# Hash attention and a gated feed-forward on one core: the feed-forward of a batch placed inside the attention of the next, with DMA transposes of the operands and weights cast by DMA

## The chip, the cores and the metric

The kernel runs on one core of one Trainium2 chip. The metric is device time in microseconds (us); less is better. A time is one execution on the chip; the median of three is given with its lowest and highest. One execution was also taken by the hardware profiler, and all durations come from that one. PE is TensorE, DVE is VectorE, ACT is ScalarE, POOL is GpSimd, SP is SyncE, from which most DMAs are issued.

## The reference, cut to what matters

Attention of 4 batches x 8 heads, 768 tokens, 64 dims; a score counts only where query and key fall into the same bucket, which is given by the signs of 6 projections. Then a gated feed-forward over all 3072 tokens.

```python
q_bits = einsum('bhsd,dk->bhsk', q, proj) > 0        # the same for k; proj is 64 x 6
mask = bucket(q_bits)[:, :, :, None] == bucket(k_bits)[:, :, None, :]
scores = where(mask, q @ k.T / sqrt(64), -1e9)
attn = softmax(scores) @ v                            # 4 x 8 x 768 x 64
x = attn.transpose(0, 2, 1, 3).reshape(3072, 512)
ffn = (gelu(x @ w_gate) * (x @ w_val)) @ w_out        # 512 -> 1536 -> 512
out = x + sigmoid(x @ w_res) * ffn
```

## The kernel before, in words

The mask costs no comparison. Six bit rows of plus or minus one half and one constant row stand under the 64 dims of each operand, so that a matmul over 71 rows gives the scaled score and, where any bit differs, a large negative amount beside it; the exponential then gives zero. The exponential's scale puts the size right, so q is divided by 2048 when it is copied.

A pair is two heads of a batch; there are 16 pairs, worked in groups of two. `prep` (L120) makes the operands of a group. For each pair and side it loads 384 KB of float32 (L128), transposes six 128x128 blocks on PE into PSUM (L137), copies them to SBUF with DVE (L139) and casts the two heads' halves into the operand tile `aug`, one half on POOL (L144) and one on DVE (L145). The values are loaded, cast to bfloat16 with a column of ones beside them, and summed over tokens on POOL (L147 to L158). Bit matmuls of all four operands of the group go to four column strips of PE (L166), DVE makes signs of them (L169), and 16 small DMAs carry seven rows each under the operands (L176).

`attn` (L189) works a pair in nine chunks. A chunk has 1024 score columns in two PSUM banks (L212), one exponential of 128 x 1024 (L217) and eight value matmuls of 65 columns (L230). Each head is opened by a matmul of 390 columns that adds a tiny multiple of the value sums (L223) and closed by a reciprocal and a product on DVE (L201, L202), which write `x_tok`. After each batch `xpose` transposes `x_tok` to `x_sb`, 24 blocks on PE, with copies on DVE (L242, L244).

Weights are loaded in float32 tiles on SP and cast on POOL (L94, L97), three pieces a group from the second group on. When all attention is done, the PSUM pools are closed and the feed-forward runs over six blocks of 512 tokens: for each of 12 slices of the hidden width four matmuls for the gate (L276), gelu on ACT (L279), four for the value (L282) and a product on DVE (L284); then for each 128 tokens four matmuls for the residual gate (L288), a tanh (L291), twelve output matmuls (L294), two DVE instructions (L298, L299) and a store (L301).

The order on each engine is made by a scheduler from dependences and priorities, and each engine runs its own list strictly in that order. A `tile` of a pool waits for a free buffer of its tag.

Of the kernel before, what the change touches and what calls it, by code (L numbers as in the profile page):

```python
# [18 lines left out]
def kernel(  # L19
# [12 lines left out]
    nc = tc.nc  # L32
    B, H, S, D = q.shape
    NBITS = proj.shape[1]
    NTOK = B * S
# [7 lines left out]
    NPAIR = B * HP  # L43
    NROW = NBITS + 1
    assert D == 64 and S == 768 and NBITS <= 15
# [10 lines left out]
    ident = const.tile([P, P], FP32, name="ident")  # L56
    make_identity(nc, ident)
    ident_bf = const.tile([P, P], BF16, name="ident_bf")
    nc.vector.tensor_copy(ident_bf, ident)
    eps_sb = const.tile([P, P], BF16, name="eps_sb")  # L60
    nc.vector.memset(eps_sb, EPS)

    projw = const.tile([P, 32], FP32, name="projw")
    nc.vector.memset(projw, 0.0)
    nc.sync.dma_start(projw[0:D, 0:NBITS], proj)
    nc.sync.dma_start(projw[D:2 * D, NROW:NROW + NBITS], proj)

    cst = const.tile([P, 1], FP32, name="cst")
    nc.gpsimd.memset(cst, -0.5)
    for j in range(4):  # L70
        for hi in range(2):
            nc.gpsimd.affine_select(
                out=cst, in_=cst, compare_op=ALU.not_equal,
                fill=(1.0 if j % 2 == 0 else -NBITS / 4.0),
                base=-(32 * j + hi * NROW + NBITS), pattern=[[0, 1]], channel_multiplier=1)

    x_tok = const.tile([P, B * T, DMODEL], BF16, name="x_tok")
    x_sb = const.tile([P, KM, NTOK], BF16, name="x_sb")

    w_pool = ctx.enter_context(tc.tile_pool(name="w", bufs=1))  # L80
    wst_pool = ctx.enter_context(tc.tile_pool(name="wst", bufs=2))
    wts = {}

    def load_w(ap, kdim, ndim, name):
        t = w_pool.tile([P, kdim // P, ndim], BF16, name=name)
        wts[name] = t
        per = DFF // ndim
        todo = []
        for k0 in range(0, kdim // P, per):
            n = min(per, kdim // P - k0)  # L90

            def go(k0=k0, n=n):
                tmp = wst_pool.tile([P, per, ndim], FP32, tag="wtmp", name="wtmp")
                nc.sync.dma_start(  # L94
                    tmp[:, :n, :],
                    ap[k0 * P:(k0 + n) * P, :].rearrange("(o p) n -> p o n", p=P))
                nc.gpsimd.tensor_copy(t[:, k0:k0 + n, :], tmp[:, :n, :])  # L97
            todo.append(go)
        return todo

    wload = (load_w(moe_w_gate, DMODEL, DFF, "wg") + load_w(moe_w_val, DMODEL, DFF, "wv")
             + load_w(moe_w_res, DMODEL, DMODEL, "wr") + load_w(moe_w_out, DFF, DMODEL, "wo"))

    with ExitStack() as actx:
        ld_pool = actx.enter_context(tc.tile_pool(name="ld", bufs=3))
        aug_pool = actx.enter_context(tc.tile_pool(name="aug", bufs=4))
        t32_pool = actx.enter_context(tc.tile_pool(name="t32", bufs=5))
        va_pool = actx.enter_context(tc.tile_pool(name="va", bufs=4))
        bit_pool = actx.enter_context(tc.tile_pool(name="bit", bufs=2))
        e_pool = actx.enter_context(tc.tile_pool(name="e", bufs=12))  # L110
        sm_pool = actx.enter_context(tc.tile_pool(name="sm", bufs=2))
        misc_ps = actx.enter_context(tc.tile_pool(name="misc_ps", bufs=2, space=PSUM))
        sc_ps = actx.enter_context(tc.tile_pool(name="sc_ps", bufs=2, space=PSUM))
        av_ps = actx.enter_context(tc.tile_pool(name="av_ps", bufs=2, space=PSUM))

        CH = [(0, 4), (4, 2)]
        KA = D + NROW
        vaug, aug = {}, {}
# [213 lines left out]
```

## Time and profile before

| | us |
|---|---|
| median of 3 runs | 423.8 |
| lowest, highest | 420.07, 426.41 |
| the profiled execution | 423.37 |
| its span, first to last instruction | 421.1 |

Mean granted TensorE clock over the span: 0.986 of 2.4 GHz. The profile gives each engine's busy time, groups of instructions by line and shape, the waits, and the chain of work that ended last. Ends of matmuls are modelled and overlap with the next ones, so a rate of PE is read from the starts. The idle time behind a row, with the engine that ended it, stands in brackets.

### The profile page before, as it was taken

How to read it: one execution, taken by the hardware profiler on the slowest of the kernel's cores; microseconds unless marked ns; L12 is line 12 of the kernel's file. 1: busy time of each engine (PE TensorE's matmuls, PEld its weight loads, DVE VectorE, ACT ScalarE, POOL GpSimd, SP SyncE). 2: the span in 40 equal slices, each digit the busy share in tenths (PEclk: the TensorE clock that was granted, in tenths of full speed). 3: DMA queues.
4: the chain of work that ended last, by engine and by line, in shares of the span. 5: the costliest groups of instructions: out<-in, count | busy, mean ns of one | idle time of the engine just before them, and what ended most of it. 6: DMA issues, size and time to landing. Idle time of an engine off the chain costs nothing.

```text
span 421.1 us, 7282 instructions
## 1 busy us (share of the span) xinstructions
PE 381.9 (91%) x2924; PEld 199.4 (47%) x2944; DVE 184.3 (44%) x315; ACT 200.2 (48%) x242; POOL 101.2 (24%) x157
## 2 busy tenths in 40 slices
PE   1788988879989898989799999999999999999995
PEld 1454555645565456545444444444444444444442
DVE  1674362936355274631234433344343334334433
ACT  1008879587977768789643123223213313312321
POOL 4961662835558362720000000000000000000000
PEclk9999999999999699999899999999999999999999
DMA  7802728348184732300000110010020010011001
GB/s 244 279 8 86 263 83 297 104 141 298 37 296 158 239 141 86 112 10 2 2 0 0 51 51 2 25 75 2 5 81 15 0 76 25 0 52 50 1 27 75
DMA packets 23138, 36.82 MB, mean 87 GB/s; under 512 B 4672, under 2 KB 16960, under 8 KB 23104
## 3 DMA queue, kind: packets, MB, share of 16 engines
q1 hardware_dynamic: 23104, 36.35, 24.9%
q8 instruction: 23, 0.38, 0.4%
q14 instruction: 11, 0.09, 0.1%
HBM read 29.36 MB, written 6.29 MB: 85 GB/s over the span
## 4 chain that ended last, share of the span: by engine, by line
PE 67%; ACT 10%; DVE 8%; DMA 5%; issue 4%; POOL 3%; SPq 2%; ACTq 0%; DVEq 0%; POOLq 0%
PE gps L276 15%; PE vps L282 15%; PE fps L294 15%; ACT e L217 10%; PE sp L212 6%; PE av L230 5%; PE rps L288 5%; DVE t L139 3%; DVE aug L145 3%; PE tp L137 3%; DMA wtmp<-in_moe_w_out_dram 2%; PE hs L166 2%; DMA ld<-in_k_dram 2%; DMA ld<-in_q_dram 1%; SPq L176 1%
## 5 line engine op out<-in xcount | busy, mean ns | idle before, releaser
L217 ACT ACTIVATE e<-sp 128x1024 bf16<-128x1024 f32 x144 | 140.4, 1021 | 63.6 <-PE sp L212 59.4
L212 PE MATMUL sp<-aug,aug 71*128 71x256 bf16 (+1 forms) x384 | 86.9, 332 | 0.0
L279 ACT ACTIVATE gt<-gps 128x512 bf16<-128x512 f32 x72 | 43.0, 597 | 88.5 <-PE gps L276 85.1
L284 DVE TENSOR_TENSOR hh<-gt,vps 128x512 bf16<-128x512 bf16 x72 | 49.5, 687 | 74.0 <-PE vps L282 67.0
L230 PE MATMUL av<-va,e 128*128 128x65 bf16 x1152 | 61.7, 196 | 14.5 <-ACT e L217 10.5
L276 PE MATMUL gps<-x_sb,wg 128*128 128x512 bf16 x282 | 73.9, 383 | 0.3
L282 PE MATMUL vps<-x_sb,wv 128*128 128x512 bf16 x283 | 73.2, 379 | 0.3
L230 PEld LDWEIGHTS <-e 128*128 128x128 bf16 x1152 | 46.3, 99 | 53.7 <-ACT e L217 49.0
L294 PE MATMUL fps<-wo,hh 128*128 128x512 bf16 x281 | 65.5, 379 | 0.4
L139 DVE TENSOR_SCALAR t<-tp 128x512 f32<-128x512 f32 x64 | 32.8, 550 | 28.1 <-PE tp L137 24.8
L276 PEld LDWEIGHTS <-wg 128*128 128x128 bf16 x288 | 28.4, 99 | 34.6 <-issue 1.1
L144 POOL CAST aug<-t 64x768 bf16<-64x768 f32 x32 | 33.9, 1063 | 45.1 <-DVE t L139 24.9
L282 PEld LDWEIGHTS <-wv 128*128 128x128 bf16 x288 | 28.2, 98 | 34.3 <-issue 0.5
L294 PEld LDWEIGHTS <-hh 128*128 128x128 bf16 x288 | 28.2, 98 | 34.0
L291 ACT ACTIVATE th<-rps 128x512 f32<-128x512 f32 x24 | 14.3, 597 | 61.7 <-PE rps L288 58.9
L137 PE MATMUL tp<-ident,ld 128*128 128x128 f32 x192 | 33.9, 314 | 7.6 <-DMA ld<-in_q_dram 3.9
L298 DVE SCALAR_TENSOR_TENSOR o<-th,fps 128x512 f32<-128x512 f32 x24 | 16.5, 687 | 52.4 <-PE fps L294 49.6
L212 PEld LDWEIGHTS <-aug 71*128 71x128 bf16 x384 | 29.3, 99 | 8.4 <-issue 1.0
L137 PEld LDWEIGHTS tp<-ident,ld 128*128 128x128 f32 x192 | 25.7, 161 | 14.0 <-DVE t L139 6.8
L201 DVE RECIPROCAL rec<-av 128x6 f32<-128x6 f32 x32 | 6.1, 192 | 54.9 <-PE av L230 54.9
L145 DVE CAST aug<-t 64x768 bf16<-64x768 f32 x32 | 28.9, 904 | 2.6 <-PE sp L212 1.7
L288 PE MATMUL rps<-wr,x_sb 128*128 128x512 bf16 x94 | 25.1, 387 | 0.3 <-issue 0.2
(34 smaller groups left out, 186.9 us busy)
## 6 DMA issues: line engine op xcount, KB each, us to landing
ld<-in_q_dram SPq DMA_DIRECT2D x16, 384.0 KB
ld<-in_k_dram SPq DMA_DIRECT2D x16, 384.0 KB
ldv<-in_v_dram SPq DMA_DIRECT2D x16, 384.0 KB
out_dram<-o SPq DMA_DIRECT2D x24, 256.0 KB
wtmp<-in_moe_w_gate_dram SPq DMA_DIRECT2D x4, 768.0 KB
wtmp<-in_moe_w_val_dram SPq DMA_DIRECT2D x4, 768.0 KB
wtmp<-in_moe_w_out_dram SPq DMA_DIRECT2D x4, 768.0 KB
aug<-bits SPq DMA_DIRECT2D x64, 10.5 KB
```

The costliest lines, as they stand in the source:

```text
L137: nc.tensor.transpose(ps[:, bass.ts(c, P)], s[:, hi, bass.ts(tp, P)], ident)
L139: nc.vector.tensor_scalar_mul(tt[:, c0 * P:(c0 + n) * P], ps[:, :n * P], (1.0 / C) if side == 0 else 1.0)
L145: nc.vector.tensor_copy(ag[0:D, :, 1, :], t3[D:2 * D])
L212: nc.tensor.matmul(sp[:, off:off + nq * P], ks[hi][:, bass.ts(jt, P)], qs[hi][:, qt0 * P:(qt0 + nq) * P], start=True, stop=True)
L217: nc.scalar.activation(e, sp, AF.Exp, scale=float(ALPHA))
L230: nc.tensor.matmul(av[hi][:, qt, :], e[:, off:off + P], va[:, hi, jt, 0:D + 1], start=False, stop=(jt == T - 1), skip_group_check=True)
L276: nc.tensor.matmul(gps, wg[:, kk, bass.ts(m, P)], xr[:, kk, :], start=(kk == 0), stop=(kk == KM - 1))
L279: nc.scalar.activation(gt, gps, AF.Gelu)
L282: nc.tensor.matmul(vps, wv[:, kk, bass.ts(m, P)], xr[:, kk, :], start=(kk == 0), stop=(kk == KM - 1))
L284: nc.vector.tensor_mul(hh[:, m, :], gt, vps)
L288: nc.tensor.matmul(rps, xr[:, kk, bass.ts(tt, P)], wr[:, kk, :], start=(kk == 0), stop=(kk == KM - 1))
L294: nc.tensor.matmul(fps, hh[:, m, bass.ts(tt, P)], wo[:, m, :], start=(m == 0), stop=(m == KF - 1))
```

## The change

- Operands are no longer transposed on PE. q and k are cast (POOL, the very first on ACT) in their natural layout into one of four fixed tiles `nat`, 128 tokens x 12 blocks x 128 columns, of which 64 are the dims, seven the bits and the constant, and the rest zeros.
- The bits are made from 32x32 block transposes on DVE (four strips of 32 tokens side by side), matmuls with the projection on four column strips, one DVE block transpose back, and four DVE instructions for each operand that write the signs into `nat`.
- One DMA transpose for each operand, on SP, turns `nat` into `aug`. `x_sb` is also made by DMA transposes, one for each pair, from its `finish`.
- Weights are loaded by POOL's DMAs, which cast from float32 to bfloat16, in 12 pieces.
- The feed-forward works on one batch (768 tokens). `gate_val` of a batch stands as one block after the first four chunks of the next batch; `project` is cut into 30 pieces, of which one follows each chunk, and the last six are held back for the four chunks ahead of the next block. Gate and value use the PSUM buffers of the scores, `project` and the bits share two others. The last batch's feed-forward stands behind all attention.
- The value matmuls of a chunk follow the scores of the next chunk. At the start PE runs 14 matmuls on constants, and pairs 0 and 1 are prepared one by one.

The core of the difference:

```diff
+    def load_w():
+        if wload:
+            nc.gpsimd.dma_start(*wload.pop(0))
...
+    def cast(x, eng):
+        scale = (1.0 / C) if x[1] == 0 else 1.0
+        dst = nat_of(x)[:, :, 0:D]
+        if eng is nc.scalar:
+            nc.scalar.activation(dst, raw[x], AF.Copy, scale=scale)
+        elif x[1] == 0:
+            eng.tensor_scalar(dst, raw[x], scale, 1.0, op0=ALU.mult, op1=ALU.mult)
+        else:
+            eng.tensor_copy(dst, raw[x])
...
+    def prep(ps, first=False):
+
+        jobs = [(p, side) for p in ps for side in range(2)]
+        n = 32 * len(jobs)
+        hs = mm_ps.tile([P, HT, 32], FP32, tag="mm", name="hs")
+        for i, x in enumerate(jobs):
+            cast(x, nc.scalar if first and i == 0 else nc.gpsimd)
+        yield
+        for h in range(2):
+            t32 = []
+            for x in jobs:
+                tt = t32_pool.tile([P, T, 2, 32], FP32, tag="t32", name="t32")
+                nc.vector.transpose(tt.rearrange("p c h n -> p (c h n)"),
+                                    raw[x][:, h * T:(h + 1) * T].rearrange("p c d -> p (c d)"))
...
+            for dh in range(2):
+                for j, tt in enumerate(t32):
+                    nc.tensor.matmul(hs[32 * j:32 * j + 32, h * T:(h + 1) * T, :],
+                                     projw[:, dh, :], tt[:, :, dh, :],
+                                     start=(dh == 0), stop=(dh == 1),
+                                     tile_position=(0, 32 * j))
+            yield
+        ht = sm_pool.tile([P, HT, 32], FP32, tag="ht", name="ht")
+        nc.vector.transpose(ht[:n].rearrange("p c n -> p (c n)"),
+                            hs[:n].rearrange("p c n -> p (c n)"))
+        for j, x in enumerate(jobs):
+            del raw[x]
+            for a in range(4):
+                nc.vector.tensor_scalar(
+                    nat_of(x)[32 * a:32 * a + 32, :, D:D + NBITS],
+                    ht[32 * j:32 * j + 32, :, NBITS * a:NBITS * (a + 1)], 0.0, 0.5,
+                    op0=ALU.is_gt, op1=ALU.subtract)
+            ag = aug_pool.tile([P, HT, P], BF16, tag=f"aug{x[1]}", name=f"aug{x[1]}")
+            nc.sync.dma_start_transpose(out=ag, in_=nat_of(x).rearrange("p c n -> p (c n)"))
+            aug[x] = ag
+            yield
...
+    def finish(p, hi):
...
+        if hi == 1:
+            nc.sync.dma_start_transpose(out=x_sb[b][:, hp],
+                                        in_=x_tok[b][:, hp].rearrange("p t n -> p (t n)"))
...
+    def gate_val(b):
+        hh = hh_pool.tile([P, KF, S], BF16, tag="hh", name="hh")
+        hidden[b] = hh
+        xs = x_sb[b].rearrange("p k t n -> p k (t n)")
+        for m in range(KF):
+            ps = []
+            for w in (wg, wv):
                 sp = sc_ps.tile([P, 1024], FP32, tag="sp", name="sp")
...
+                for kk in range(KM):
+                    for c0, c1 in ((0, 512), (512, S)):
+                        nc.tensor.matmul(sp[:, c0:c1], w[:, kk, bass.ts(m, P)],
+                                         xs[:, kk, c0:c1],
+                                         start=(kk == 0), stop=(kk == KM - 1))
+                ps.append(sp)
+                if w is wg:
+                    gt = g_pool.tile([P, S], BF16, tag="gt", name="gt")
+                    nc.scalar.activation(gt, sp[:, 0:S], AF.Gelu)
+            nc.vector.tensor_mul(hh[:, m, :], gt, ps[1][:, 0:S])
...
+    for g in range(NG):
+        b, half = divmod(g, HP // 2)
+        side = prep((2 * g + 2, 2 * g + 3)) if g + 1 < NG else iter(())
+        for s in range(2 * NCH):
+            p, c = 2 * g + s // NCH, s % NCH
+            scores(p, c)
+            if s == 0 and g + 2 < NG:
+                load(2 * g + 4)
+            if s == NCH and g + 2 < NG:
+                load(2 * g + 5)
+            if s in (3, 6, 9, 12, 15) and g < 3:
+                load_w()
+            next(side, None)
+            if b >= 1:
+                slot = half * 2 * NCH + s
+                if slot < LEAD:
+                    mlp_piece()
+                    mlp_piece()
+                elif slot > LEAD and mlp and mlp[0][1] < 5 * T - HELD:
+                    mlp_piece()
+                if slot == LEAD - 1:
+                    flush()
+                    while mlp:
+                        mlp_piece()
+                    gate_val(b - 1)
+                    mlp.append([project(b - 1), 0])
+        run(side)
+    flush()
+    while mlp:
+        mlp_piece()
+    gate_val(B - 1)
+    run(project(B - 1))
```

How the scheduler's lists change is shown at two places. On ACT, before, from the first exponential on; `e` is the exponential of a chunk, `th` the tanh, `gt` the gelu:

```order
L217 ACT_TABLE_LOAD
L217 ACTIVATE e<-sp 128x1024 x144
L291 ACTIVATE th<-rps 128x512
L279 ACT_TABLE_LOAD
L279 ACTIVATE gt<-gps 128x512 x12
L291 ACTIVATE th<-rps 128x512 x3
```

And ACT after, from the first exponential to the middle of the second batch:

```order
L260 ACTIVATE e<-sp 128x1024 x40
L282 ACT_TABLE_LOAD
L282 ACTIVATE gt<-sp 128x768
L296 ACTIVATE th<-rps 128x512
L282 ACTIVATE gt<-sp 128x768 x11
L260 ACT_TABLE_LOAD
L260 ACTIVATE e<-sp 128x1024 x7
L296 ACTIVATE th<-rps 128x512
```

All 144 exponentials stood ahead of the first gelu; now 40 do, and each of four blocks of gelus stands between exponentials or behind them, with a change of the activation table at either edge.

On SP at the start, before, around the first group's bits; `ld` are loads of q and k, `aug` the operands:

```order
L147 DMA ldv<-in_v_dram 128x2x384
L128 DMA ld_623<-in_q_dram 128x2x384
L128 DMA ld_639<-in_k_dram 128x2x384
L176 DMA aug_152<-bits 7x6x128 x2
L176 DMA aug_168<-bits 7x6x128 x2
```

And SP after, at the same place; `ld_144` and `ld_146` are the first pair, `ld_199` and `ld_201` the third, `nat` the natural operands:

```order
L120 DMA ld_195<-in_k_dram 128x2x384
L125 DMA ldv<-in_v_dram 128x2x384
L120 DMA ld_199<-in_q_dram 128x2x384
L191 DMA_TRANSPOSE aug_175<-nat_68 128x12x128
L191 DMA_TRANSPOSE aug_181<-nat_71 128x12x128
L120 DMA ld_201<-in_k_dram 128x2x384
L120 DMA ld_248<-in_q_dram 128x2x384
L120 DMA ld_250<-in_k_dram 128x2x384
L125 DMA ldv<-in_v_dram 128x2x384
L191 DMA_TRANSPOSE aug_230<-nat_74 128x12x128
```

The small bit DMAs stood behind the loads of five pairs' q and k; now the first pair's transposes stand behind the loads of two pairs and one q, and the third pair's k stands behind the transposes.

## Rows read from the trace of the kernel before

**Rows 1.** The page: busy time of the engines; the closing chain by engine.

```profile
PE 381.9 (91%) x2924; PEld 199.4 (47%) x2944; DVE 184.3 (44%) x315; ACT 200.2 (48%) x242; POOL 101.2 (24%) x157
...
PE 67%; ACT 10%; DVE 8%; DMA 5%; issue 4%; POOL 3%; SPq 2%; ACTq 0%; DVEq 0%; POOLq 0%
```

**Rows 2.** Busy time by stretch, with clock, DMA share and GB/s.

```profile
core 0: us, PE busy (x) PEld busy (x) DVE busy (x) ACT busy (x) POOL busy (x), PEclk, DMA share, GB/s
0.00:31.50 31.50, 18.39 (x86) 11.04 (x87) 16.90 (x31) 1.28 (x1) 21.88 (x48) 1.00 0.54 178
31.50:206.00 174.50, 154.94 (x1886) 93.51 (x1884) 83.45 (x162) 140.35 (x144) 79.35 (x109) 0.98 0.42 142
206.00:421.10 215.10, 208.59 (x954) 94.88 (x974) 83.91 (x123) 58.60 (x98) 0.00 (x0) 0.99 0.08 30
...
180.00:206.00 26.00, 22.44 (x288) 12.38 (x287) 5.61 (x14) 24.90 (x26) 1.58 (x3) 1.00 0.02 5
...
300.00:340.00 40.00, 39.79 (x183) 18.15 (x186) 15.28 (x23) 10.75 (x18) 0.00 (x0) 1.00 0.08 29
```

**Rows 3.** Groups by line and shape: busy us, mean ns | idle before, releaser.

```profile
L217 ACT ACTIVATE e<-sp 128x1024 bf16<-128x1024 f32 x144 | 140.4, 1021 | 63.6 <-PE sp L212 59.4
...
L284 DVE TENSOR_TENSOR hh<-gt,vps 128x512 bf16<-128x512 bf16 x72 | 49.5, 687 | 74.0 <-PE vps L282 67.0 <-ACT gt L279 3.9 <-PE gps L276 3.1
...
L279 ACT ACTIVATE gt<-gps 128x512 bf16<-128x512 f32 x72 | 43.0, 597 | 88.5 <-PE gps L276 85.1 <-PE vps L282 3.4
...
L139 DVE TENSOR_SCALAR t<-tp 128x512 f32<-128x512 f32 x32 | 22.0, 688 | 27.2 <-PE tp L137 23.9 <-POOL wr L97 2.1 <-POOL aug L144 0.7
...
L139 DVE TENSOR_SCALAR t<-tp 128x256 f32<-128x256 f32 x32 | 13.2, 413 | 0.9 <-PE tp L137 0.9
...
L201 DVE RECIPROCAL rec<-av 128x6 f32<-128x6 f32 x32 | 6.1, 192 | 54.9 <-PE av L230 54.9
...
L279 ACT ACT_TABLE_LOAD x1 | 1.3, 1283 | 0.0
```

**Rows 4.** Timelines: ACT alone, the last attention chunks, gate and value, projections.

```profile
182.66 23.35 ACT L217 ACTIVATE e<-sp 128x1024 bf16<-128x1024 f32 x23
...
203.12 0.42 PE L230 MATMUL av<-va,e 128*128 128x65 bf16 x8 [0.26 <-ACT e L217]
...
203.37 0.60 PE L212 MATMUL sp<-aug,aug 71*128 71x256 bf16 x3
...
212.85 1.03 PE L282 MATMUL vps<-x_sb,wv 128*128 128x512 bf16 x4
...
213.98 0.69 DVE L284 TENSOR_TENSOR hh<-gt,vps 128x512 bf16<-128x512 bf16 x1 [0.91 <-PE vps L282]
...
410.55 2.75 PE L294 MATMUL fps<-wo,hh 128*128 128x512 bf16 x12
...
413.14 1.03 PE L288 MATMUL rps<-wr,x_sb 128*128 128x512 bf16 x4
```

**Rows 5.** Timeline of the start: first load, first PE work, bits, first exponential.

```profile
0.73 0.44 SPq L128 DMA_DIRECT2D ld<-in_q_dram  x1
...
3.88 1.51 PE L137 MATMUL tp<-ident,ld 128*128 128x128 f32 x6 [3.88 <-DMA ld<-in_q_dram]
...
28.76 2.18 PE L166 MATMUL hs<-t,projw 128*32 128x512 f32 x16 [0.43 <-DVE t L139]
...
31.52 1.94 ACT L217 ACTIVATE e<-sp 128x1024 bf16<-128x1024 f32 x2 [29.50 <-PE sp L212]
```

**Rows 6.** SP's time on DMAs: ns min/median/max, of a load and of bits.

```profile
L128 SPq DMA_DIRECT2D ld<-in_q_dram x16: 368/468/1090, 0.7 to 165.8; - x16
...
L176 SPq DMA_DIRECT2D aug<-bits x64: 777/778/1001, 21.4 to 185.4; - x64
```

**Rows 7.** Timeline of the end: the last output matmuls and DVE instruction.

```profile
414.00 2.75 PE L294 MATMUL fps<-wo,hh 128*128 128x512 bf16 x11
...
417.57 0.69 DVE L299 SCALAR_TENSOR_TENSOR o<-o,x_tok 128x512 f32<-128x512 f32 x1
```

More of the change, by code (lines that the diff above doesn't have):

```diff
@@ L68 @@
[L68 to L78, printed above, removed]
@@ new lines @@
+    projw = const.tile([P, 2, 32], FP32, name="projw")
+    nc.vector.memset(projw, 0.0)
+    for a in range(4):
+        nc.scalar.dma_start(projw[32 * a:32 * a + 32, :, NBITS * a:NBITS * (a + 1)],
+                            proj.rearrange("(h r) n -> r h n", r=32))
+    eps_sb = const.tile([P, P], BF16, name="eps_sb")
+    nc.gpsimd.memset(eps_sb, EPS)
+    warm = const.tile([P, 512], BF16, name="warm")
+    nc.gpsimd.memset(warm, 0.0)
+    NN = 4
+    nat = []
+    for i in range(NN):
+        nat.append(const.tile([P, HT, P], BF16, name=f"nat{i}"))
+        eng = nc.vector if i < 2 else nc.gpsimd
+        eng.memset(nat[i][:, :, D:P], 0.0)
+        eng.memset(nat[i][:, :, D + NBITS:KA], 1.0 if i % 2 == 0 else -NBITS / 4.0)
@@ new lines, in values @@
+    def values(p, c, e):
+        va, vsum = vaug[p]
+        for i in range(2):
+            hi, parts = banks[2 * c + i]
+            if (p, hi) not in av:
+                o = av_ps.tile([P, T, D + 1], FP32, tag="av", name="av")
+                av[p, hi] = o
+                nc.tensor.matmul(
+                    o, eps_sb,
+                    vsum[:, hi, 0:D + 1].unsqueeze(1).to_broadcast([P, T, D + 1]),
+                    start=True, stop=False, skip_group_check=True)
+            off = i * 512
+            for (jt, qt0, nq) in parts:
+                for qt in range(qt0, qt0 + nq):
+                    nc.tensor.matmul(av[p, hi][:, qt, :], e[:, off:off + P],
+                                     va[:, hi, jt, 0:D + 1],
+                                     start=False, stop=(jt == T - 1), skip_group_check=True)
+                    off += P
+            if (2 * c + i + 1) % NCH == 0:
+                finish(p, hi)
@@ new lines, with flush, scores @@
+    pending = []
+    def flush():
+        while pending:
+            values(*pending.pop(0))
+    def scores(p, c):
+        qs, ks = aug[p, 0], aug[p, 1]
+        sp = sc_ps.tile([P, 1024], FP32, tag="sp", name="sp")
+        for i in range(2):
+            hi, parts = banks[2 * c + i]
+            off = i * 512
+            for (jt, qt0, nq) in parts:
+                nc.tensor.matmul(sp[:, off:off + nq * P], ks[0:KA, hi * T + jt, :],
+                                 qs[0:KA, hi * T + qt0:hi * T + qt0 + nq, :],
+                                 start=True, stop=True)
+                off += nq * P
+        e = e_pool.tile([P, 1024], BF16, tag="e", name="e")
+        nc.scalar.activation(e, sp, AF.Exp, scale=float(ALPHA))
+        flush()
+        pending.append((p, c, e))
@@ new lines, with run, mlp_piece @@
+    wps = mm_ps.tile([P, 512], FP32, tag="mm", name="wps")
+    for i in range(14):
+        nc.tensor.matmul(wps, eps_sb, warm, start=True, stop=True)
+    def run(gen):
+        for _ in gen:
+            pass
+    load(0)
+    run(prep((0,), first=True))
+    load(1)
+    load(2)
+    run(prep((1,)))
+    load(3)
+    NG = NPAIR // 2
+    LEAD = 4
+    HELD = 6
+    mlp = []
+    def mlp_piece():
+        while mlp:
+            g = mlp[0]
+            try:
+                next(g[0])
+                g[1] += 1
+                return
+            except StopIteration:
+                mlp.pop(0)
```

324 lines of the change are left out of this document (110 added, 214 removed).

## The prediction

> **What bounds the kernel now.** I read the page's shares first, then busy time by stretch, then the groups by shape, then timelines of three places. The page gives PE 91% of the span and 67% of the closing chain, ACT 10% [rows 1]. The stretches split that average into three stages [rows 2]. Up to 31.5 us no exponential has run. From 31.5 to 206 us is the attention, 174.5 us for 144 exponentials, ACT 140.4 us busy, PE 154.9. From 206 us on is the feed-forward, 215.1 us, where PE is busy 39.79 of 40 us and ACT about 11. So the last stage is PE alone, and the middle one neither engine alone: at its undisturbed end (180 to 206 us) ACT is busy 24.90 of 26 us, before that it waits for scores behind preparation work. Busy PE there is the pipelines' length and not the rate, so I take rates from starts [rows 4]: twelve matmuls of 512 columns run from 410.55 to 413.14, 216 ns each; eight value matmuls from 203.12 to 203.37, 0.25 us; 23 exponentials in 23.35 us, 1.015 us each. A chunk (1024 score columns, eight value matmuls) is thus 0.43 + 0.25 us of PE, with the 390-column opening matmul of each head (one in 4.5 chunks, 0.04) 0.72 us, against 1.015 us of ACT. The attention leaves PE some 30% free; the feed-forward leaves ACT about 70% free. That is the room the fusion uses.
>
> **The change part by part.** The profiled execution took 423.37 us, 2.3 us above its span, and stands at the median of the three runs (423.8). I sum the span of the new kernel.
>
> *Start.* Now the first exponential ends 29.50 us of idle ACT [rows 5], because both pairs of the first group pass PE and DVE by turns and their bits go out together. After: one pair. Its q lands at 3.9 us [rows 5], k some 0.5 us behind. Four DVE transposes of 384 columns: between the 256- and 512-column rows (413 and 688 ns [rows 3]) about 0.55 each, 2.2 us. Bit matmuls: at most the 2.18 us of today's group [rows 5]; I take 1.3. One more transpose and eight bit instructions, at the 192 ns of the smallest DVE row [rows 3]: 2.1 us. That is 10 us. Then two DMA transposes in a row on SP, then scores.
>
> No trace here shows a DMA transpose. One moves 384 KB, 1536 pieces of 256 bytes. The lower bound is a load of the same size, 0.73 to 3.88 us from issue to use [rows 5], and 0.47 us of SP's time [rows 6]. The upper is the small DMA that today carries bits, also in 256-byte pieces: 777 ns of SP for 42 of them [rows 6], so 28.4 us for 1536. I take the load, which it resembles in bytes and partitions: 3.2 us each, one after the other, 6.4. Scores and their exponential follow 1 us on: first exponential at 18 us (14 if the two transposes overlap, 68 at the upper bound).
>
> The Trainium skill speaks against this part: "VectorE: DVE Perf Modes", section "The three transpose paths", has 1309 ns for one 128x128 block by DMA against 390 ns on TensorE. Twelve blocks at that are an estimate of 15.7 us. The Trainium skill's "DMA: Bandwidth & Descriptors", section "Latency and other measured facts", has 261 GB/s for transposes, an estimate of 1.5 us for the same bytes. By the first the third rival comes true, by the second the sum stands; the trace has no such DMA to decide it.
>
> *First batch, no feed-forward beside it.* 36 chunks and the four of the next batch ahead of its feed-forward, ACT-bound: 40 x 1.015 = 40.6 us. The DMA engines must bring, before the first feed-forward, 18 loads of 384 KB (7.1 MB), eight weight slices of 768 KB (6.3), the residual weights (1.0) and 12 large and three half-size transposes (5.3): 19.7 MB. The start moved 178 GB/s at a share of 0.54 [rows 2], 330 GB/s at full share, so 60 us, as long as start and chunks together (58.6). A transpose waits on SP for its bits, and behind it in that queue stands the third pair's k load; that pair's first bit matmuls stand in PE's queue ahead of and among the first scores, so PE waits for those loads. I add 5 us for both: the first feed-forward starts at 63.6 us.
>
> *From there PE is the bound.* Feed-forward, unchanged in columns (six blocks of 160 matmuls before): 960 x 216 ns = 207.4 us, of which gate and value 124.4 and projections 82.9. The other 104 chunks x 0.72 = 74.9 us. Bits of the five groups left, 5 x 2.18 = 10.9 us. Gone from PE are 192 + 96 transposes; DVE and POOL lose the copies behind them, which are under other work. Sum 293.2 us.
>
> *Frictions.* Gate and value share two PSUM buffers. DVE starts 0.27 us after the last value column (212.85 + 0.86 to 213.98 [rows 4]); for 768 columns it takes 687 + 256 x 1.07 = 962 ns [rows 3]: 1.23 us, just inside the next gate's 1.30. Cover gone, every 0.1 us over costs 48 x 0.1 = 5 us. Projection pieces between chunks share two buffers with the bits: 5% of the 168.8 us of mixed work, 8.4 us. Each batch's last tokens reach the feed-forward through a DMA transpose (half size); four chunks or six held pieces cover it, and I charge 1.5 us x 4 = 6.
>
> *Table loads.* Six more, 1283 ns each [rows 3]. A gelu of 768 columns lies halfway between 597 ns for 512 and 1021 ns for 1024 [rows 3], 0.81 us. At an entry the first one ends 1.28 + 0.81 = 2.1 us after the last exponential, while PE has 0.25 + 1.3 + 1.3 = 2.85 us to do before it needs that buffer; at an exit PE has two chunks' scores and nine projection matmuls (2.8 us) against 2.3. Nothing on the path. The Trainium skill's "ScalarE: Activation LUTs", section "What ACT_TABLE_LOAD costs", gives 2.7 us with the drain and advises grouping by set; by it entries would wait 0.65 us, exits 0.9, and the sum would be 5 us higher. The trace's 1283 ns decides here.
>
> *End.* The last matmul is issued at 414.00 + 2.59 = 416.6 us of 421.1 [rows 7]; the same 4.5 us follow.
>
> Sum: 63.6 + 293.2 + 8.4 + 6 + 4.5 = 375.7, with 2.3 outside the span **378 us**.
>
> **Rivals.** *Data late.* If casting weight loads and transposes run at half the rate, 12.6 MB at 165 GB/s and 7.1 at 330 take 98 us; the first feed-forward starts 34 us later, 412 us, and halfway 395. For it: the start alone has a share of 0.54. Against: over the attention it is 0.42, with the same loads and weights in it [rows 2].
>
> *In-order stalls.* All 144 exponentials need 146.2 us by rate and took 174.5 [rows 2, 4], a factor of 1.19, because PE's queue held preparation ahead of scores. The same on the 168.8 us of mixed work costs 32 us in place of 8.4: 402 us. Against: most of what held it (PE transposes and their DVE round trips) is gone.
>
> *The transpose queue is the bound, slower than before.* All 32 large and 16 half-size transposes stand in SP's order, 40 equivalents. At t each they need 40t, with 11 us ahead of the first and 56 us of feed-forward and end behind the last: 40t + 67 us. It decides from t = 8.9 us, where that is 423; at the upper bound of 28.4 it is 1203 us. Loads and output stores stand behind each, and PE would idle at every batch. For it: SP's time on 256-byte pieces [rows 6]. Against: those DMAs span seven partitions, and a load that spans 128 takes SP 0.47 us for 36 times the bytes [rows 6].
>
> **How the numbers follow.** Forecast 378 us: 0.56. Data late: 0.15. Stalls: 0.11. Both together, 415 to 432 us, no change that a measurement could tell (about 2% is what it can): 0.07. Transpose queue: 0.11. Faster is the first three, 0.82; same 0.07; slower 0.11. Low end: start at 14 us (-4), no late data (-5), no frictions (-14.4), bits in half the time (-5): 350, taken as 352. High end 414, past the far end of late data, which leaves the last two cases and little else out.
>
> **What would show it.** Right: first exponential near 18 us; about one exponential per us to some 64 us; then PE at 216 ns per 512 columns in four blocks of about 31 us, and ACT waiting for PE, not PE for ACT, in the mixed parts; SP's time on a transpose below 4 us. Wrong: PE waiting for DMA at the head of the first block (data late); PE idle before projection matmuls for DVE or ACT (stalls); SP busy without a gap and scores waiting for transposes (queue).

## The result, and the profile after

The changed kernel takes 407.5 us (median of four runs, 406.5 to 409.75) against 424.0 for the kernel before (four runs): ratio 0.965, 95% interval 0.957 to 0.973. It is faster, but by 3.5%, where 378 us (11%) was forecast. The profiled execution took 406.82 us, its span 404.7, 2.1 us less than the time; the forecast span was 375.7.

The page of the kernel after: busy time of PE, two lines of the 40 slices (10.1 us each), and the DMA queues that answer for q0 (POOL's casting loads) and q1 (SP's). It answers to [rows 1].

```profile
PE 366.9 (91%) x2944; PEld 202.2 (50%) x2990; DVE 170.7 (42%) x366; ACT 206.9 (51%) x225; POOL 81.5 (20%) x149
...
PEclk9759555865999999999999999999999999999999
DMA  7999999996910048776000973920008221100012
...
q1 hardware_dynamic: 79488, 40.91, 44.7%
q0 software_dynamic: 6336, 5.24, 8.7%
```

PE is at 91% again, but the slices show two kernels in one: ten slices at a reduced clock with the DMA engines full, then thirty at full clock. Busy time by stretch, against [rows 2], cuts at the first exponential (22.8 us), the first gate matmul (98) and the end of the first block of gate and value (132):

```profile
core 0: us, PE busy (x) PEld busy (x) DVE busy (x) ACT busy (x) POOL busy (x), PEclk, DMA share, GB/s
0.00:22.80 22.80, 10.85 (x52) 4.45 (x53) 11.10 (x32) 2.12 (x2) 12.95 (x28) 0.84 1.01 225
22.80:40.00 17.20, 13.80 (x132) 6.77 (x130) 10.31 (x28) 10.82 (x11) 11.30 (x20) 0.80 1.11 260
40.00:60.00 20.00, 16.47 (x117) 8.29 (x118) 4.85 (x12) 8.49 (x9) 6.60 (x11) 0.50 1.30 200
60.00:80.00 20.00, 19.16 (x164) 9.01 (x163) 10.64 (x30) 11.30 (x12) 8.72 (x16) 0.66 1.20 239
80.00:98.00 18.00, 13.27 (x110) 6.66 (x109) 7.94 (x25) 9.29 (x10) 7.54 (x12) 0.60 0.95 204
98.00:132.00 34.00, 32.83 (x203) 19.75 (x205) 12.01 (x14) 11.88 (x16) 5.12 (x8) 0.96 0.46 100
132.00:176.00 44.00, 42.53 (x448) 24.21 (x454) 20.58 (x50) 34.79 (x37) 9.46 (x19) 1.00 0.57 117
```

The forty exponentials that were to take 40.6 us (and 5 of waits) take 75.4. Between 40 and 60 us only nine run; the granted clock is 0.50, the 1.2 GHz level, the DMA share (mean busy share of 16 engines; overlapping packets take it above 1) is 1.30. Timeline of ACT and PE at five places of that stage, with the idle time in brackets:

```profile
22.81 1.94 ACT L260 ACTIVATE e<-sp 128x1024 bf16<-128x1024 f32 x2 [17.85 <-PE sp L255]
...
57.50 1.02 ACT L260 ACTIVATE e<-sp 128x1024 bf16<-128x1024 f32 x1 [4.65 <-PE sp L255]
...
88.13 1.02 ACT L260 ACTIVATE e<-sp 128x1024 bf16<-128x1024 f32 x1 [5.64 <-PE sp L255]
89.42 1.02 ACT L260 ACTIVATE e<-sp 128x1024 bf16<-128x1024 f32 x1 [0.27 <-PE sp L255]
...
98.18 0.83 PE L276 MATMUL sp<-x_sb,wg 128*128 128x512 bf16 x2
```

ACT waits 4 to 6 us for scores here and there, and between the holes a chunk often takes 1.29 us (88.13 to 89.42) at the lower clock. From here on, *the stage* is the time from the first exponential to the first gate matmul. Behind it the timeline of ACT has twelve gelus in a block, from the third on (107.67) 2.60 us apart, and the exponentials' table back at 131.90:

```profile
128.47 0.81 ACT L282 ACTIVATE gt<-sp 128x768 bf16<-128x768 f32 x1 [1.79 <-PE sp L276]
131.07 0.81 ACT L282 ACTIVATE gt<-sp 128x768 bf16<-128x768 f32 x1 [1.79 <-PE sp L276]
131.90 1.28 ACT L260 ACT_TABLE_LOAD   x1
```

Groups by line and shape, against [rows 3]:

```profile
L260 ACT ACTIVATE e<-sp 128x1024 bf16<-128x1024 f32 x144 | 144.4, 1022 | 83.8 <-PE sp L255 82.4
...
L283 DVE TENSOR_TENSOR hh<-gt,sp 128x768 bf16<-128x768 bf16 x48 | 45.8, 953 | 81.1 <-PE sp L276 81.1
...
L168 DVE STREAM_TRANSPOSE t<-ld 128x384 f32<-128x384 f32 x64 | 33.8, 557 | 43.8 <-DMA ld<-in_q_dram 21.3 <-PE hs L175 14.7 <-DMA ld<-in_k_dram 7.6
...
L282 ACT ACT_TABLE_LOAD x4 | 5.1, 1283 | 0.1
```

The new operation, the DMA transpose of an operand: SP's time on it (min, median, max in ns), who waits for it, its time from issue to landing; then, from SP's timeline, two of the first stage and four late in the kernel. It answers to [rows 6].

```profile
L191 SPq DMA_TRANSPOSE aug<-nat x32: 1437/1832/6596, 11.8 to 310.0; - x32
...
  POOL nat L138: 73.8, 10
...
DMA to landing us min/median/max: 3.7/4.9/11.8
```

```profile
50.13 10.44 SPq L191 DMA_TRANSPOSE aug<-nat  x2
...
304.92 7.01 SPq L191 DMA_TRANSPOSE aug<-nat  x4
```

Late in the kernel a transpose holds SP for 1.75 us (7.01 for four), and the quickest landed in 3.7; in the first stage two hold it for up to 10.44 us, and one lands after as much as 11.8.

### The profile page after: what moved, and what is told of

Its sections match the earlier page's. It is cut to its first block, busy times and chain, and to the rows that moved or that the text cites. A ratio compares the mean times of both kernels' runs of the same rounds, so it can differ in the third digit from the quotient of the medians.

```text
span 404.7 us, 7265 instructions
## 1 busy us (share of the span) xinstructions
PE 366.9 (91%) x2944; PEld 202.2 (50%) x2990; DVE 170.7 (42%) x366; ACT 206.9 (51%) x225; POOL 81.5 (20%) x149
## 3 DMA queue, kind: packets, MB, share of 16 engines
q0 software_dynamic: 6336, 5.24, 8.7%
## 5 line engine op out<-in xcount | busy, mean ns | idle before, releaser
L255 PE MATMUL sp<-aug,aug 71*128 71x256 bf16 (+1 forms) x384 | 98.2, 362 | 4.3 <-DMA aug<-nat 4.1
L282 ACT ACTIVATE gt<-sp 128x768 bf16<-128x768 f32 x48 | 38.9, 810 | 83.3 <-PE sp L276 83.3
L283 DVE TENSOR_TENSOR hh<-gt,sp 128x768 bf16<-128x768 bf16 x48 | 45.8, 953 | 81.1 <-PE sp L276 81.1
L276 PE MATMUL sp<-x_sb,wg 128*128 128x512 bf16 (+1 forms) x382 | 72.0, 328 | 2.6 <-DMA x_sb<-x_tok 2.1
L276 PE MATMUL sp<-x_sb,wv 128*128 128x512 bf16 (+1 forms) x371 | 70.0, 324 | 1.2 <-DVE hh L283 0.5
L168 DVE STREAM_TRANSPOSE t<-ld 128x384 f32<-128x384 f32 x64 | 33.8, 557 | 43.8 <-DMA ld<-in_q_dram 21.3
L175 PE MATMUL hs<-t,projw 128*32 128x192 f32 x256 | 27.3, 375 | 17.8 <-DVE t L168 11.7
L186 DVE TENSOR_SCALAR nat<-ht 32x72 bf16<-32x72 f32 x128 | 31.3, 244 | 2.3
L138 POOL TENSOR_SCALAR nat<-ld 128x768 bf16<-128x768 f32 x15 | 12.4, 829 | 73.8 <-DMA aug<-nat 73.8
L145 POOL CAST va<-ldv 128x768 bf16<-128x768 f32 x16 | 13.2, 822 | 57.2 <-PE av L235 52.5
## 6 DMA issues: line engine op xcount, KB each, us to landing
ld<-in_q_dram SPq DMA_DIRECT2D x16, 384.0 KB, 4.7
ld<-in_k_dram SPq DMA_DIRECT2D x16, 384.0 KB, 4.6
ldv<-in_v_dram SPq DMA_DIRECT2D x16, 384.0 KB, 5.0
wg<-in_moe_w_gate_dram POOLq DMA_DIRECT2D x4, 384.0 KB, 9.6
wv<-in_moe_w_val_dram POOLq DMA_DIRECT2D x4, 384.0 KB, 7.1
wo<-in_moe_w_out_dram POOLq DMA_DIRECT2D x3, 512.0 KB, 10.7
```

Of the source, the lines that this page charges most:

```text
L168: nc.vector.transpose(tt.rearrange("p c h n -> p (c h n)"), raw[x][:, h * T:(h + 1) * T].rearrange("p c d -> p (c d)"))
L175: nc.tensor.matmul(hs[32 * j:32 * j + 32, h * T:(h + 1) * T, :], projw[:, dh, :], tt[:, :, dh, :], start=(dh == 0), stop=(dh == 1), tile_p ...
L186: nc.vector.tensor_scalar(nat_of(x)[32 * a:32 * a + 32, :, D:D + NBITS], ht[32 * j:32 * j + 32, :, NBITS * a:NBITS * (a + 1)], 0.0, 0.5, o ...
L255: nc.tensor.matmul(sp[:, off:off + nq * P], ks[0:KA, hi * T + jt, :], qs[0:KA, hi * T + qt0:hi * T + qt0 + nq, :], start=True, stop=True)
L276: nc.tensor.matmul(sp[:, c0:c1], w[:, kk, bass.ts(m, P)], xs[:, kk, c0:c1], start=(kk == 0), stop=(kk == KM - 1))
L282: nc.scalar.activation(gt, sp[:, 0:S], AF.Gelu)
```

## The experiments

Four theories on the first stage were put against each other: A, the amount of DMA time ahead of the first feed-forward sets its start; B, TensorE's half clock does; C, the order in SP's queue does; D (added after e1 to e4), late data makes TensorE wait, and the clock that falls in the waits adds as much again. Three points of the span tell the runs apart, from the timelines:

| run | time, us | first exponential | first gate matmul | table of the exponentials back | from there to the end |
|---|---|---|---|---|---|
| changed kernel | 406.8 | 22.8 | 98.2 | 131.9 | 272.8 |
| e1 third of weights, constants | 399.8 | 26.1 | 91.7 | 125.2 | 272.5 |
| e2 plain copies | 393.5 | 20.3 | 86.6 | 119.9 | 271.5 |
| e3 two fill matmuls | 406.1 | 22.6 | 90.6 | 128.1 | 276.0 |
| e4 late output weights | 415.4 | 22.5 | 95.1 | 140.8 | 272.9 |
| e5 third of weights | 392.7 | 23.0 | 84.2 | 118.1 | 272.8 |
| e6 e5 with plain copies | 386.2 | 21.0 | 81.4 | 113.4 | 271.0 |
| e7 TensorE transposes, 12 operands | 387.8 | 20.2 | 75.8 | 108.4 | 277.5 |
| e8 e7 with third of weights | 384.0 | 20.3 | 77.3 | 109.9 | 272.4 |
| e9 e7, paired | 386.3 | 20.9 | 74.7 | 107.5 | 276.7 |
| e10 TensorE transposes, all | 399.1 | 19.8 | 71.9 | 104.5 | 292.8 |
| e12 one fill matmul | 415.3 | 22.3 | 96.4 | 138.7 | 274.6 |

Each row is one profiled execution; the changed kernel and e9 were timed four times (406.5 to 409.75 and 381.0 to 386.3 us), the others once. e1 to e4, e5 to e8 and e9 to e12 ran on three chips, where the kernel before took 425.3, 418.6 and 419.2 us, so a difference of a few us between two rows shows nothing by itself. From the return of the exponentials' table on, all but e10 take 271 to 278 us: what the runs differ by lies ahead of it.

**e1.** Edit:

```diff
+    wload = wload[:2]
-    for s in range(3):
+    for s in range(1):
...
+    nc.gpsimd.memset(wg[:, :, DFF // NS:], 0.01)
```

> Left out: eight of the twelve weight pieces are not loaded; the rest of w_gate, w_val and w_out is the constant 0.01. That takes about 23 us of DMA-engine time (two thirds of the 35 us that the casting weight loads take) out of the first stage. Theory A (the time of the 16 DMA engines bounds the stage up to the first feed-forward): the first gate matmul comes at 72 to 78 us in place of 98, the time is 382 to 388 us. Theory B (TensorE's half clock sets the pace of the first stage): the clock is not touched at its cause, first gate matmul at 92 to 98 us, 402 to 407 us. Theory C (the order in SP's queue, not the amount, sets it): the weights do not go through SP's queue, so the same as B.

The gate matmul came at 91.7, just ahead of B's and C's numbers and far from A's; the time, 399.8, lies between A's and theirs. But the constants disturbed the run. Timelines of DVE and POOL in it:

```profile
10.09 11.30 DVE L187 TENSOR_SCALAR nat<-ht 32x72 bf16<-32x72 f32 x8
...
13.51 3.96 POOL L328 MEMSET wv<- 128x4608 bf16 x1
```

Eight bit instructions of the first pair took 11.30 us beside POOL's long writes; in the changed kernel the same eight take 3.02. So the first exponential came 3.3 us later, and e5 repeats the experiment without the constants.

**e2.** Edit:

```diff
-            nc.sync.dma_start_transpose(out=ag, in_=nat_of(x).rearrange("p c n -> p (c n)"))
+            nc.sync.dma_start(out=ag, in_=nat_of(x))
```

> Left out: the transposition of the operands; the same 384 KB go from nat to aug by plain DMA copies in the same place of SP's queue, and the exponential's scale is 0.001 so that it stays finite. Theory A: a copy in 256-byte or longer pieces takes about 1.2 us of all DMA engines in place of about 2.6, so 11 to 12 copies give back 12 to 16 us: first gate matmul at 82 to 88 us, 390 to 396 us. Theory B: 98 us and 407 as before, unless the chunks come faster. Theory C: the copies stand at the same places in the queue and wait for the same bits, so at most 3 us.

86.6 and 393.5: inside A's numbers, far from B's and C's. SP's queue has the same order, so the order alone (C) is not the cause. But A is not singled out by it: the copies changed what an operand costs SP much more than when it landed. SP's rows and the time from issue to landing, from 20 to 98 us, of the changed kernel and of e2:

```profile
L191 SPq DMA_TRANSPOSE aug<-nat x12: 1450/3509/6596, 22.0 to 93.6; - x12
...
DMA to landing us min/median/max: 3.8/7.3/11.8
```

```profile
L191 SPq DMA_DIRECT2D aug<-nat x13: 465/475/600, 19.7 to 87.6; - x13
...
DMA to landing us min/median/max: 2.8/7.2/9.1
```

The loads of q and k stand behind the operands in SP's queue, and from 22 to 86 us DVE waited 17.0 us for them in the changed kernel, 3.2 in e2. (From 22 to 76 us alone the median landing is 9.9 and 7.8 us.) So e2 may owe its gain to SP, which is free sooner, as much as to the DMA engines.

**e3 and e12.** Edit of e3; e12 has one in place of two:

```diff
+        if p < HP:
+            for i in range(2):
+                nc.tensor.matmul(sp[:, 0:512], eps_sb, warm, start=True, stop=True)
```

> Nothing left out. Added: two matmuls of 512 columns on constants ahead of the scores of each of the 36 chunks of the first batch, so that TensorE is not idle long enough to lose its clock. Theory A: the granted clock of the first stage rises above 0.9, but the first gate matmul stays at 96 to 101 us and the time at 405 to 411 us. Theory B: the clock rises and the first gate matmul comes 15 to 25 us earlier, at 73 to 83 us, 382 to 392 us. Theory C: as A.

> Nothing left out. One matmul of 512 columns on constants ahead of each chunk of the first batch, instead of two: TensorE's work for a chunk is then 0.72 + 0.22 = 0.94 us at the full clock, below the exponential's 1.02, so that the filling costs nothing by itself. Theory D: the clock stays up more than in the changed kernel, first gate matmul at 86 to 93 us, 396 to 403 us, and the waits for data grow as they did with two. Theory A: 96 to 99 us, 405 to 408 us. Theory B: 72 to 82 us, 380 to 391 us.

Busy time by stretch of e3, then of e12, for the two stretches in which the changed kernel has clocks of 0.50 and 0.66:

```profile
40.00:60.00 20.00, 16.25 (x150) 8.64 (x151) 3.88 (x10) 10.57 (x11) 8.44 (x14) 0.83 1.26 212
60.00:80.00 20.00, 13.47 (x150) 7.36 (x150) 8.37 (x30) 11.15 (x11) 7.47 (x14) 0.95 1.16 252
```

```profile
40.00:60.00 20.00, 13.08 (x101) 6.79 (x99) 2.85 (x8) 7.16 (x7) 6.60 (x11) 0.67 1.29 180
60.00:80.00 20.00, 14.44 (x147) 7.35 (x145) 4.51 (x10) 9.80 (x10) 7.80 (x14) 0.84 1.25 196
```

The clock rose to 0.83 and 0.95 (e3), 0.67 and 0.84 (e12), and ACT spent 21.7 and 17.0 us on exponentials in these 40 us, against 19.8 in the changed kernel. B as the whole cause falls: TensorE, the filling included, was busy 29.7 of these 40 us in e3 against 35.6, so at the higher clock it mostly waits longer for the same data. A share of the clock remains: e3's gate matmul came 7.6 us earlier, and in the changed kernel twelve exponentials follow the one before after 1.29 to 1.36 us in place of 1.02. The filling takes TensorE's time too, so these runs do not size that share. e12's gate matmul is A's number; its 415.3 us lie outside all three. Waits of PE, for 22 to 91 us of e3, then for 96 to 139 us of e12:

```profile
PE sp L258 <- DMA aug<-nat: 7.3, 2, 4.0
PE av L228 <- DVE x_tok L215: 5.8, 1, 5.8
```

```profile
PE sp L279 <- DMA x_sb<-x_tok: 5.5, 1, 5.5
```

Behind the gate matmul PE then waited for the last transpose of `x_sb`: 3.5 us in e3, and in e12 5.5, more than the 1.8 us won. e12 ended 9 us behind e3: it lost 5.8 us up to the gate matmul and 4.8 in the block behind it; why is not settled.

**e4.** Edit, with the slots of the last pieces moved behind the first batch:

```diff
+            if len(wload) < 4:
+                nc.gpsimd.tensor_copy(dst[:, 0, 0:1], last_e[-1][:, 0:1])
```

> Nothing left out. The four pieces that project needs (w_res and the three of w_out, about 14 us of DMA-engine time) are held back by a tiny POOL copy that reads an exponential of their place in the order, and the last three stand behind the first batch. Theory A: the first gate matmul comes 9 to 14 us earlier, at 84 to 89 us, 393 to 399 us, if the pieces land before project asks for them. Theory B and C: 96 to 99 us, 405 to 408 us.

A miss for A: 3 us earlier in place of 9 to 14, and the time rose to 415.4. The four pieces were issued at 90.7 to 96 us, just when the last `x_sb` transposes were due; PE waited 6.0 us for one inside the block. With these four pieces out of it, some 14 us of DMA time, the stage was only 2.8 us shorter, so the sum of DMA time alone did not set it; and moving a load is not taking it away.

**e5 and e6.** Edit of e5; e6 adds that of e2:

```diff
-                        nc.tensor.matmul(sp[:, c0:c1], w[:, kk, bass.ts(m, P)],
+                        nc.tensor.matmul(sp[:, c0:c1], w[:, kk, bass.ts(m % 3, P)],
```

> Left out: eight of the twelve weight pieces; gate_val uses the first quarter of w_gate and w_val over and over, project the first third of w_out, so that nothing is written in their place (the constants of the first experiment took 11.4 us of POOL, and DVE's bit instructions beside them slowed down). Theory A (amount of DMA time alone): 23 us less ahead of the first feed-forward, first gate matmul at 75 to 79 us, 384 to 388 us. Theory D (late data makes TensorE wait, some 16 us, and the waits drop its clock to half, some 18 us more; the weights only share the DMA engines with what is late): a part of it, first gate matmul at 84 to 91 us, 393 to 400 us.

> Left out: eight of the twelve weight pieces, as in the run before, and the transposition of the operands (plain copies, exponential's scale 0.001). Theory A: 23 + 12 us less DMA time; the chunks' own pace of 1.02 us becomes the limit, first gate matmul at 62 to 68 us, 372 to 378 us. Theory D: the waits go, the clock stays up for most of the stage: first gate matmul at 66 to 74 us, 376 to 384 us. If the half clock has a cause of its own (Theory B), it stays at half for 30 us or more and the gate matmul comes after 78 us.

e5 gives 14 us at the gate matmul, inside D's numbers and well short of A's 23. What became faster is the operands' landing. The DMA view for 22 to 76 us, median us to landing, of the changed kernel and of e5:

```profile
q0 software_dynamic: 4543, 3.87, 49.2%
...
aug<-nat SPq DMA_TRANSPOSE x8, 9.9
```

```profile
q0 software_dynamic: 528, 0.52, 6.2%
...
aug<-nat SPq DMA_TRANSPOSE x10, 4.8
```

The weights slow the transposes: 9.9 us with the casting loads at 49% of the engines' time, 4.8 with them at 6%. In e6 the gate matmul came at 81.4 us, later than A (62 to 68) and D (66 to 74) had it. B's "after 78 us" was met, but not its condition of 30 us at half the clock: 0.60 from 20 to 30 us, 0.61 from 60 to 70, and 0.84 or more in the other ten-us stretches up to 80. e2's 11.6 us and e5's 14 do not add, together they give 16.8; so they act for the most part on the same waits, and 60 us for 40 chunks remain. What holds these is not shown; the DMA share is still 0.82 from 40 to 60 us.

**e7 to e9.** Edit of e7, for pairs 0 to 5; in e9 these lines follow the bits of the next operand:

```diff
+        for x in jobs:
+            for h in range(2 if x[0] < NPE else 0):
+                tp = mm_ps.tile([P, T, P], BF16, tag="mm", name="tp")
+                for c in range(T):
+                    nc.tensor.transpose(tp[:, c, :], nat_of(x)[:, h * T + c, :], ident_bf)
+                nc.vector.tensor_copy(aug[x][:, h * T:(h + 1) * T, :], tp)
```

> Nothing left out. The twelve operands of pairs 0 to 5 are transposed on TensorE (twelve bf16 blocks each into two PSUM tiles) and copied to aug by DVE, the later ones by DMA as before. Takes 12 x 2.56 = 31 us of DMA time out of the first stage, adds about 12 us of TensorE time and 24 x 0.9 = 22 us of DVE time that stands in no chain of chunks. Theory A: first gate matmul at 70 to 76 us, 378 to 386 us. Theory D: the same direction, more if the added transposes keep TensorE from waiting: 68 to 78 us, 377 to 388 us. Theory B alone: granted clock up by the added work, DMA share irrelevant: the same time as A, told apart by the clock. Against all: the new transposes stand in TensorE's order behind DVE's bits, and if scores wait behind them the stage is no shorter than 90 us.

> Left out: eight of the twelve weight pieces. The operands of pairs 0 to 5 are transposed on TensorE. Ahead of the first feed-forward the DMA engines then carry the loads and some 12 us of weights only, no operand transposes. Theory A: DMA far from a bound, pace of the chunks: first gate matmul at 62 to 68 us, 371 to 377 us. Theory D: 64 to 70 us, 372 to 379 us, and at most 4 us less than with all weights. If it equals the run with all weights, the weights cost nothing once the transposes are off the DMA engines.

> Nothing left out. As the run with the operands of pairs 0 to 5 transposed on TensorE, but the transposes of an operand follow the bits of the next operand instead of all bits of the group, so that TensorE waits for 0.8 us of bits rather than for 3 to 5.6 us of them. Theory D (late data and the clock that falls in the waits): what is left of the first stage, 55.6 us for 40 chunks, shrinks by the two holes of 2 to 6 us in front of the transposes: first gate matmul at 70 to 75 us, 382 to 388 us. If the holes have another cause, first gate matmul at 75 to 78 us and 386 to 390 us. Either way faster than both kernels.

e7's gate matmul, at 75.8 us, is inside A's numbers and D's; its time, 387.8, is inside D's and 1.8 us above A's. So e7 does not part A from D. e8 decides what the weights are worth then: two thirds less of them change the gate matmul from 75.8 to 77.3. They cost nothing there once the operands are off the DMA engines (the time is 3.8 us shorter, behind the block). Both theories had its gate matmul too early (62 to 70): the stage is 55.6 us in e7, 57.0 in e8, 53.8 in e9 and 52.1 in e10, which transposes the first twelve operands as e9 does.

e9 against the kernel before: 384.9 us (381.0 to 386.3, four runs) against 419.2 (seven runs), ratio 0.916, interval 0.908 to 0.923. It beats the kernel before, and by the ratios (0.965 for the changed kernel, intervals apart) that one too. Its gate matmul came only 1.1 us before e7's, where its two cases meet, so what the holes were worth stays open. Page and stretches of e9:

```profile
PEclk9798899999999999989999999999999999999999
```

```profile
20.00:40.00 20.00, 17.12 (x206) 11.31 (x205) 18.24 (x49) 11.29 (x12) 13.49 (x23) 0.84 1.05 222
40.00:60.00 20.00, 18.48 (x245) 10.56 (x244) 12.21 (x34) 15.92 (x17) 12.13 (x23) 0.96 1.22 229
```

The DMA share is still 1.22 from 40 to 60 us, with loads and weights; but 17 exponentials run there in place of nine. A full DMA is not the limit as such; a full DMA in the chain of bits, transpose and scores is. That chain has a second turn: POOL casts into four `nat` tiles, and from 22.8 to 98.2 us of the changed kernel its casts waited 25.0 us for DMA transposes to free one. From 20 to 40 us e9 has 12 exponentials, as the changed kernel has 11 from 22.8 on: DVE is busy 18.24 of 20 us with the preparation of three pairs in a row.

**e10.** The limit of e9's edit set to all pairs.

> Nothing left out. As the run before, but all 32 operands are transposed on TensorE, none by DMA. The 20 later ones cost TensorE 20 x 0.68 = 13.6 us and DVE 20 x 1.1 = 22 us in the mixed part. If TensorE bounds that part, as forecast: 12 to 16 us slower than the run before, 396 to 404 us, and the DMA transpose is worth its price there. If the DMA engines or SP's queue had a share in that part: within 3 us of the run before or faster.

399.1 us, 14 above e9's median, as expected from TensorE's time. Groups of e10, and of e9:

```profile
L195 PE MATMUL tp<-ident_bf,nat 128*128 128x128 bf16 x384 | 34.1, 228 | 13.4 <-DVE aug L196 5.1 <-DVE ident_bf L69 3.6 <-POOL va L152 2.1
```

```profile
L195 PE MATMUL tp<-ident_bf,nat 128*128 128x128 bf16 x144 | 13.0, 237 | 8.5 <-DVE ident_bf L69 3.5 <-DVE aug L196 3.5 <-DVE nat L203 1.5
```

240 more transposes; behind the first block, where TensorE bounds, the span grows by 16.1 us, from 276.7 to 292.8, and TensorE's busy time there by 13.7. There the DMA transpose is worth its price.

**e11.** Edit:

```diff
-            if b >= 1:
-                slot = half * 2 * NCH + s
...
+    for b in range(B):
+        gate_val(b)
+        run(project(b))
```

> Nothing left out. The fusion alone is undone: all attention first, then the four batches' feed-forward one after the other; operands, DMA transposes, cast weights and block sizes stay as in the changed kernel (x tiles for four batches, one output tile instead of two to make room). Forecast by its own terms: first 40 chunks as in the changed kernel, to 98 us; the other 104 at the exponential's pace, 1.03 to 1.10 us each with the bits, 107 to 114 us; then 207.4 us of feed-forward and 4.5 us of end: span 417 to 424, time 419 to 428 us. So the fusion gives 12 to 21 us, less frictions. If the time is within 4 us of the changed kernel, the gain did not come from the fusion but from the rest.

440.2 us in one execution: the fusion gives some 33 us, more than expected (12 to 21), and without it the rest of the change makes the kernel slower than before (419.2 on that chip). Busy time by stretch of e11, from 98 us to its first gelu at 223.7:

```profile
98.00:150.00 52.00, 45.48 (x509) 22.56 (x508) 26.74 (x75) 37.31 (x38) 20.09 (x36) 0.87 0.90 210
150.00:200.00 50.00, 42.17 (x504) 21.57 (x503) 19.66 (x60) 42.26 (x45) 12.66 (x24) 0.97 0.66 123
200.00:223.00 23.00, 19.70 (x246) 9.92 (x245) 3.77 (x10) 22.12 (x24) 0.00 (x0) 1.00 0.09 19
```

With all attention in a row, an exponential takes 1.37 us while the DMA share is 0.90, 1.11 at 0.66, and its own 1.02 when nothing is loaded. I had counted 1.03 to 1.10. Preparation in the engines' queues ends where the loads end, so this does not tell which of the two stretched the exponentials. The feed-forward takes 438.4 - 223.7 = 214.7 us, close to 207.4 and 4.5.

## Why the prediction was right and wrong

*The first batch* is the step that failed. It had the DMA engines bring 19.7 MB at 330 GB/s in 60 us, as long as start and chunks, and so charged them no wait but 5 us. The DMA view up to 98 us has:

```profile
DMA packets 38359, 22.06 MB, mean 225 GB/s; under 512 B 25296, under 2 KB 38352, under 8 KB 38352
```

Two things were wrong in that sum. It counted what the first feed-forward needs, not what stands in the queues by then: nine pairs' loads and all twelve weight pieces came. And the rate came from loads, with 1.3 KB to a packet (5.60 MB in 4360); with transposes in it, two thirds of the packets are under 512 bytes. The view counts a casting load by the two bytes that it writes for each number (5.24 MB in all); counted by the four that it reads, as the forecast did, 27.3 MB in 98 us are 279 GB/s, in place of 19.7 at 330. That they are read shows in the page: 18.9 MB of q, k and v and 10.5 of weights.

```profile
HBM read 29.37 MB, written 6.29 MB: 88 GB/s over the span
```

Transposes by themselves, from 306.2 to 313 us, move 211 GB/s with the engines full:

```profile
DMA packets 5705, 1.44 MB, mean 211 GB/s; under 512 B 5705, under 2 KB 5705, under 8 KB 5705
```

But a sum of bytes over a rate is not what failed in the end: e4, e5 and e8 took weights out of the stage and won 2.8, 14 and no us of it, where the DMA time taken away was 14 and, twice, 23. What failed is the overlap: the forecast laid the DMA work under the chunks at a price of 5 us, while the chunks' own operands wait for it, and the stage took 75.4 us in place of 45.6.

The rival *data late* (0.15) gave 98 us for the first gate matmul and 412 in all; measured were 98.2 and 407.5, with the remainder 5.6 us better than forecast. It was right that late data held the first stage. That it met 98 is in part luck: it came from 19.7 MB with a part at half the rate, and its sign, PE waiting for DMA at the head of the first block, did not show; from 98 to 132 us PE has no wait for a DMA, it had waited inside the stage. By e5, e7 and e9 the DMA transposes of the operands, slowed by casting loads, are the larger part of what this stage took too long: 21.6 us of 29.8, by e9's 53.8 us for the 40 chunks in place of 75.4. Two paths lead from such a transpose to late scores, its own landing and its hold on SP's queue with the next loads behind it (e2); no run parts them. e3 and e12 show that the low clock is not the cause by itself. What holds the last 8 us, the 54 us that e9 still needs for 40 chunks, was not taken apart; DVE at 18.24 of 20 us at the stage's start speaks for the preparation of three pairs at once, which the 5 us were too little for.

*Start*: first exponential at 22.8, not 18 (its own terms give 17.4). The first transpose was issued at 11.8, not 10, and from there to the first scores, at 21.7, went 9.9 us, where the forecast had 6.4 for the two in a row; the two held SP for 7.9 us, with casting loads already in the DMA engines. As a price for one alone, the load's 3.2 us was near (3.7 at least, 4.9 median); under load it grows to 11.8. Of the figures that the Trainium skill gave for this, "VectorE: DVE Perf Modes", section "The three transpose paths", led to an estimate of 15.7 us and "DMA: Bandwidth & Descriptors", section "Latency and other measured facts", with 261 GB/s, to one of 1.5; the landings lie between them, and the rate measured here is 211 GB/s.

*From there PE is the bound*: right. From the first gate matmul to the end were forecast 312.1 us (375.7 - 63.6) and measured 306.5 (404.7 - 98.2). A gate and value pair takes 2.60 us, as 1.30 for each said; the product on DVE 953 ns for 962; the mixed part runs at full clock, PE busy 42.53 of 44 us. So the remainder was counted 5.6 us too long; the 14.4 us for frictions are the likeliest place, which no run shows. e10 confirms the bound from the other side: 13.7 us more of busy TensorE there made it 16.1 us longer.

*Table loads*: right. Seven changes of 1283 ns each stand in the groups with 0.1 us of idle time ahead of the four for the gelu; at the exit two exponentials follow the load at once: the last gelu of the first block ends at 131.88, the next exponential starts at 133.19, 1.31 us in all. From 98 us on PE waited 1.0 us for ACT in all. *End*: forecast 4.5; after, the last output matmul is issued at 399.9, 4.8 us before the end (both read as twelve intervals behind the first of twelve matmuls; eleven give 4.7 and 5.0).

*The other rivals.* In-order stalls with a factor of 1.19 did not appear in the mixed part, which ended early. In e11, where attention stands alone, the exponentials behind 98 us took 1.2 us on average, 1.18 times their rate, so outside the fused part that rival's factor is met; by which cause is open (see e11). The transpose queue as the bound needed 8.9 us for each; SP's median is 1.83 over the kernel and 3.5 in the first stage, where it may hold a part.

The sum by its terms: start +4.8, first batch +29.8, the rest -5.6: 29 us over the forecast span, which is the miss.

## What to carry to other kernels

Price a transfer by what else is in the engines when it is due, and count everything that the queues hold by then, not only what the next stage needs. An operation moved from a busy engine to the DMA engines is free only outside a chain that waits for it: here DMA transposes pay in the part that TensorE bounds (e10) and cost some 20 us in the stage that waits for data (e9), so the better kernel uses both ways. A low clock beside long waits is to be tested by filling the waits before it is blamed.

## What the runs showed of the hardware that was not expected

- Casting loads delay DMA transposes of 384 KB: a median landing of 9.9 us from 22 to 76 us, 4.8 without two thirds of the casting loads (e5), 3.7 at best. Plain copies of the same bytes are delayed too: 7.8 us (e2) and 3.1 (e6). The other way round nothing shows: without operand transposes in that window the weight pieces landed in 10.6 to 13.5 us at the median (e9), with them in 7.0 to 10.7.
- A DMA transpose of 384 KB holds SP's queue for 1.45 to 6.6 us in the first stage, a plain copy of the same bytes in the same place for 0.47 to 0.6 (e2). Transposes in a row with nothing else in the DMA engines move 211 GB/s.
- The transpose on TensorE with a copy by DVE is cheap for bf16: 24 copies of 128x768 at 543 ns in e9, and some 0.34 us of TensorE for six blocks (twelve in a row show 0.83 us, six 0.49), so about 1.8 us of engine time for an operand. "VectorE: DVE Perf Modes" of the Trainium skill, section "Rules for kernel authors", advises TensorE where PSUM will do as the destination; e9 agrees with it in the first stage, e10 speaks against it where TensorE is the bound.
- DVE's small bit instructions took 0.2 us each undisturbed (1.62 for eight, the second pair of the changed kernel) and 1.4 us beside long POOL writes (e1).
